# Moving a retention kernel's first operand work partly to GpSimd and giving weight conversions a tick per stage

## The chip, the cores and the metric

The kernel runs on one core of a Trainium2 chip. Its engines are TensorE (PE in the rows, with PEld for its weight loads), VectorE (DVE), ScalarE (ACT), GpSimd (POOL) and SyncE (SP), which here only issues DMAs. The metric is the device time of one execution in microseconds, the median of several runs.

## The reference

Three computations follow each other. First a retention layer with decay, 4 batches, 8 heads, 768 positions, head width 64; then two feed-forward layers over the 3072 resulting rows, one with a leaky ReLU and one with a sigmoid-gated activation:

```python
state = gamma * state + k[:, :, t] (x) v[:, :, t]      # for t in range(768)
y[:, :, t] = scale * q[:, :, t] @ state
x = y as (3072, 512)
h = x @ w_in;  x = maximum(0.01 * h, h) @ w_out        # 512 -> 2048 -> 512
h = x @ w2_in; x = h / (1 + exp(-1.702 * h)) @ w2_out
```

The weights come as float32 widened to 64 bits per element with the value spread over two 32-bit words, so the kernel puts each weight together on the chip before it uses it.

## The kernel before, in words

**Retention.** The 768 positions of a batch are six chunks of 128, so there are 24 steps `s` (last batch first). A step loads one megabyte of q, k and v (`a_load`, four places in turn), multiplies scores (`a_scores`: 16 matmuls at line 741, then one VectorE product with the mask at line 744), scales the keys in eight ScalarE instructions (`a_decay`, line 752), runs the products with the values and the state (`a_out`, lines 764 to 777, state update at 780) and puts the result into SBUF times the query decay (`a_store`, lines 790 and 799). `retention()` is a generator with two halves per step. The first seven steps (`N_PRO`) run alone, with `early(s)` behind each; the other 17 are fed, half a step per tick, into the first 31 ticks of the first layer.

**The layers.** Each layer has two classes. `First` does the product with `w_in` as a seven-product scheme on blocks of 384 columns: four blocks `blk`, eight weight slots `q`, seven products of six matmuls each (line 371). A product is one tick. `Second` does the product with `w_out` (line 596). The order is `first1`, `second1`, `first2`, `second2`. Each product takes one operand form of the block (`First.form`: for forms 3 and 6 a difference in `tmp`, then a rounded copy on ScalarE at line 345, then the remainder on VectorE at line 151). `early_sums` (lines 332 and 333) makes the sum `tmp` and the block difference that forms 5 and 7 need.

**Weights.** `Prep` handles half a slot: `load` (two DMAs of 256 KB, line 203 or 206), `open` (two ScalarE conversions, lines 168 and 169), three VectorE word steps (lines 172, 174 and 176), `round_up` (an integer add on GpSimd, line 185), `total` (three VectorE subtractions: one 128x256, two 128x128, line 151), and then either `keep` (split into the slot: ScalarE copy, line 154, VectorE remainder) or `store` (line 226). The first two slots of the second layer's `w_in` are split and stored as two parts (`split`, `store_split`, lines 234 and 235).

**Order.** All engines run their instructions in program order, and the program order is written by hand. `Later` holds steps by tick: `clock.at(n, step)` puts `step` behind the instructions of the n-th tick from now. `OWN_AT` gives the ticks of the sixteen `1i` preparations (each slot `q` is first needed at tick 7q up to q = 5, then at 39 and 46); `OPEN1` and `OPEN2` give the ticks at which the stored preparations begin. Raw words have two places in turn in the first ticks, then three (`prep_rings[0]`); prepared halves have three (`prep_rings[1]`), and a `split` takes a second one. `behind1` is a queue of weight splits that is worked off one per tick. Activated blocks leave through a ring of buffers `first1.g`, stored by ScalarE's DMA queue at line 383; this ring has four buffers when n is 26 or 27.

Before, the early work is VectorE's:

```python
for n, words in enumerate(EARLY_PREPS):                 # (3, 4)
    if s == words:
        own[n].own_words(later, 1, 2)                   # open + words + round_up, total, keep
...
        first1.form(0, i, (0, 0, 1), e=nc.vector)       # forms 1, 2, 5, 6 at s = 3, 4, 5, 6
...
    first1.early_sums(nc.vector)                        # s == 5
```

Of the kernel before, what the change touches and what calls it, by code (L numbers as in the profile page):

```python
# [25 lines left out]
NC = S // P  # L26
# [12 lines left out]
def _word(bits):  # L39
# [18 lines left out]
N_PRO, N_SINGLE, N_IN1 = 7, 5, 10  # L58
EARLY_LOADS = (0, 3, 4)
EARLY_PREPS = (3, 4)  # L60
EARLY_FORMS = ((1, 3), (2, 4), (5, 5), (6, 6))
OWN_AT = {2: (None, 0, 1, 2), 3: (None, 2, 1, 2), 4: (3, 6, 1, 2), 5: (5, 8, 1, 2), 6: (8, 11, 1, 2), 7: (12, 15, 1, 2),
          8: (16, 19, 1, 2), 9: (20, 23, 1, 2), 10: (23, 26, 1, 5), 11: (26, 29, 1, 3), 12: (28, 31, 1, 3),
          13: (30, 34, 2, 4), 14: (32, 37, 2, 4), 15: (35, 41, 2, 3)}
FED = [2 if k in (10, 18, 26) else 1 for k in range(31)]
OPEN1 = (*range(54, 100, 5), *range(109, 157, 5), *range(165, 195, 5))
OPEN2 = (10, 16, 22, 28, 34, 39, *range(53, 100, 8), *range(109, 158, 8), 165, 173, 181)
# [31 lines left out]
def retention_two_ffn(ctx: ExitStack, tc: tile.TileContext, qkv, consts, small, w1i, w1o, w2i, w2o, scratch, out):  # L99
# [50 lines left out]
    def subtract(o, x, y, e=nc.vector):  # L150
        e.tensor_tensor(out=o, in0=x, in1=y, op=ALU.subtract)  # L151

    def split(hi, lo, src, eng=nc.vector):
        nc.scalar.copy(out=hi, in_=src)
        subtract(lo, src, hi.bitcast(F32), eng)
# [31 lines left out]
    class Prep:  # L187
# [52 lines left out]

        def own_words(self, clock, total, keep):
            self.open()
            self.word(3)
            round_up(self.f, self.low, nc.gpsimd)
            clock.at(total, lambda: self.total(nc.vector))
            clock.at(keep, self.keep)

# [4 lines left out]
        def plan(self, clock, at, lead, keep=False):  # L252
            clock.at(at - lead, self.load)
            clock.at(at, self.open)
            clock.at(at + 1, lambda: self.word(2))
            clock.at(at + 2, self.last_word)
            clock.at(at + 4, lambda: self.total(nc.vector))
            if keep:
                clock.at(at + 6, self.keep)
            elif self.kind == "2i" and self.q < N_SPLIT:  # L260
                clock.at(at + 5, self.split)
                clock.at(at + 7, self.store_split)
            else:
                clock.at(at + 5, self.store)

# [429 lines left out]
    first1.load(0)  # L695

    def early(s):

        for n, words in enumerate(EARLY_PREPS):
            if s == words:  # L700
                own[n].own_words(later, 1, 2)
        if s in EARLY_LOADS:
            own[EARLY_LOADS.index(s) + 1].load()
        for i, k in EARLY_FORMS:
            if s == k:
                first1.form(0, i, (0, 0, 1), e=nc.vector)
        if s == NC - 1:
            first1.early_sums(nc.vector)
        later.tick()

    def retention():
# [103 lines left out]
        a_load(3)  # L815
        own[0].load()
        nc.vector.memset(idle, 0.0)
        first = few.view(3.5, 8)
# [11 lines left out]
        a_decay(0)  # L830
        a_decay(1)
        for s in range(len(steps)):
            if s == 0:
                keep_warm(6)
            elif s + 1 < len(steps):
                a_scores(s + 1)
            yield
            o = a_out(s)
            if s == 0:
                a_scores(1)  # L840
                keep_warm(6)
            put = a_store(s, o)
            if s + 2 < len(steps):
                a_decay(s + 2)
            n = s + 4 if s < 15 else s + 3
            if s != 15 and n < len(steps):
                a_load(n)
            if put is not None:
                put()
            yield  # L850
# [7 lines left out]
    behind1 = collections.deque()  # L858
    for k, i in enumerate(FORMS[4:]):
        first1.form(0, i, (2 * k, 2 * k, 2 * k + 1), e=nc.vector)  # L860
    for n, (load, words, total, keep) in OWN_AT.items():
        if load is not None:
            later.at(load, own[n].load)
        later.at(words, lambda p=own[n], a=total, b=keep: p.own_words(later, a, b))

    todo1 = names["1o"] + names["2i"][2 * N_SPLIT : N_IN1] + names["2i"][: 2 * N_SPLIT]
    assert len(todo1) <= len(OPEN1)
    for p, at in zip(todo1, OPEN1):
        p.plan(later, at, 7)

# [17 lines left out]

    def done_first(kind, second, clock, behind):
        def done(blk, q):  # L890
            if blk < 3:
                return
            if q < NQ - 2:
                w_load(kind, q, 3, 7)
                w_load(kind, q, 0, 3)
                clock.at(6, lambda: behind.extend(w_steps(q, 3, 7) + w_steps(q, 0, 3)))
                return
            w_load(kind, q, 6, 7)
            second.loads(3 if q == NQ - 2 else 5)

        return done

    first1.run(done_first("1o", second1, later, behind1), step1, behind1, chunks, N_SINGLE, FED)
    while behind1:
# [69 lines left out]
    for p, at in zip(todo, OPEN2):  # L974
        p.plan(later2, at, 5, p.kind == "2i")

# [7 lines left out]

    first2.run(done_first("2o", second2, later2, behind), step2, behind)
    while behind:
# [127 lines left out]
```

## Time and profile before

| | us |
|---|---|
| median of 3 runs | 1101.69 (1100.98 to 1101.76) |
| profiled execution, its own time | 1103.22 |
| span of that execution, first to last instruction | 1101.5 |
| PE busy | 1041.2 (95%) |
| DVE busy | 823.8 (75%) |
| ACT busy | 620.1 (56%) |
| POOL busy | 139.6 (13%) |

The profiled execution spends 1.7 us outside its span and is 1.5 us longer than the median of the runs. In that execution the seven lone retention steps last until about 40 us, the fed steps until about 150, `first1` until 390, `second1` until 619, `first2` until 867, and `second2` to the end. A busy share is an average over these stages, so each stage is read by itself. PE's busy time also counts matmuls that run at a lower granted clock.

### The profile page before, as it was taken

What the parts mean: (1) busy time and instruction counts of PE and PEld (TensorE: products, weight loads), DVE (VectorE), ACT (ScalarE), POOL (GpSimd) and SP (SyncE); (2) the same over time, 40 slices, a digit from 0 to 9 for tenths busy, and PEclk for the clock granted to TensorE, in tenths of its full rate; (3) what the DMA queues carried; (4) which work ended last, traced back from release to release, by engine and by line L of the source; (5) the groups of instructions that cost most, each with busy time, mean ns of one, the idle gap of its engine ahead of it and who ended that gap; (6) DMA issues with size and microseconds to landing.
All of it is one profiled execution on the core that took longest, in us unless ns stands there. A gap on an engine that the chain in (4) does not pass through costs nothing.

```text
span 1101.5 us, 17557 instructions
## 1 busy us (share of the span) xinstructions
PE 1041.2 (95%) x6150; PEld 925.6 (84%) x6151; DVE 823.8 (75%) x1351; ACT 620.1 (56%) x1223; POOL 139.6 (13%) x97
## 2 busy tenths in 40 slices
PE   8788988999996999999999998999999999999998
PEld 5567778899996978888888997999999888888886
DVE  5987676778685679788788776556575699798886
ACT  4564654566575655455455665555567655544543
POOL 0110023333331000000000012232220000000000
PEclk9899998999998999999999998999999999999999
DMA  9679954787979873632726673766779752834724
GB/s 341 210 240 329 289 184 136 240 294 255 357 241 340 270 250 96 201 106 86 253 82 228 217 256 124 252 222 225 253 232 326 240 183 63 220 103 111 195 77 77
DMA packets 190568, 231.37 MB, mean 210 GB/s; under 512 B 59152, under 2 KB 146192, under 8 KB 187408
## 3 DMA queue, kind: packets, MB, share of 16 engines
q1 hardware_dynamic: 148704, 179.08, 51.7%
q10 hardware_dynamic: 41776, 51.17, 13.0%
q8 instruction: 48, 0.79, 0.3%
q14 instruction: 40, 0.33, 0.1%
HBM read 141.46 MB, written 88.74 MB: 209 GB/s over the span
## 4 chain that ended last, share of the span: by engine, by line
PE 61%; DMA 14%; DVE 14%; ACT 4%; issue 2%; POOL 2%; SPq 1%; ACTq 1%; POOLq 0%; DVEq 0%
PE psum L596 39%; PE psum L371 20%; DMA w<-qkv 5%; DVE e L151 3%; DVE c L151 2%; DVE w L151 2%; POOL c L185 1%; DMA e<-w2o 1%; DMA e<-w2i 1%; DMA wd2o<-ex 1%; DVE ex L151 1%; PE psum L741 1%; DMA ex<-w2i 1%; DMA wds<-c 1%; DMA ex<-w1o 1%
## 5 line engine op out<-in xcount | busy, mean ns | idle before, releaser
L596 PE MATMUL psum<-c,w 128*128 128x512 f32 x1008 | 229.0, 389 | 0.0
L596 PEld LDWEIGHTS psum<-c,w 128*128 128x128 f32 x1008 | 189.1, 188 | 39.5 <-DVE c L151 0.2
L596 PE MATMUL psum<-e,w 128*128 128x512 f32 x576 | 136.1, 389 | 0.0
L371 PE MATMUL psum<-a,w 128*128 128x384 f32 x576 | 115.4, 350 | 18.5 <-ACT psum L476 8.9
L596 PEld LDWEIGHTS psum<-e,w 128*128 128x128 f32 x576 | 108.0, 188 | 22.9 <-DVE e L151 0.5
L371 PEld LDWEIGHTS psum<-a,w 128*128 128x128 f32 x576 | 104.4, 196 | 23.2 <-ACT psum L476 10.6
L371 PE MATMUL psum<-c,w 128*128 128x384 f32 x576 | 112.9, 339 | 5.9 <-DVE d L400 4.5
L371 PE MATMUL psum<-b,w 128*128 128x384 f32 x576 | 111.1, 336 | 0.4 <-ACT psum L476 0.4
L371 PEld LDWEIGHTS psum<-c,w 128*128 128x128 f32 x576 | 101.6, 190 | 8.5 <-DVE d L400 6.3
L371 PEld LDWEIGHTS psum<-b,w 128*128 128x128 f32 x576 | 101.6, 189 | 0.8 <-ACT psum L476 0.7
L549 ACT CAST c<-b 128x512 fp32r<-128x512 f32 x96 | 59.5, 622 | 55.7 <-DVE c L151 30.3
L151 DVE TENSOR_TENSOR c<-c 128x256 f32<-128x256 f32 (+2 forms) x130 | 62.0, 477 | 37.6 <-POOL c L185 28.5
L371 PE MATMUL psum<-d,w 128*128 128x384 f32 x384 | 78.9, 349 | 8.2 <-DVE w L151 5.0
L371 PE MATMUL psum<-e,w 128*128 128x384 f32 x384 | 77.3, 345 | 6.5 <-DVE dx L400 2.4
L151 DVE TENSOR_TENSOR c<-b,c 128x512 fp32r<-128x512 f32 x96 | 65.6, 690 | 20.1 <-ACT c L549 18.1
L371 PEld LDWEIGHTS psum<-d,w 128*128 128x128 f32 x384 | 68.9, 194 | 12.3 <-DVE w L151 6.0
L371 PEld LDWEIGHTS psum<-e,w 128*128 128x128 f32 x384 | 68.4, 193 | 10.5 <-DVE dx L400 3.4
L390 ACT ACTIVATE d<-psum 128x384 f32<-128x384 f32 x96 | 46.9, 489 | 50.7 <-PE psum L371 46.4
L151 DVE TENSOR_TENSOR w<-w 128x512 fp32r<-128x512 f32 (+3 forms) x102 | 50.3, 529 | 32.7 <-ACT w L285 26.2
L185 POOL TENSOR_TENSOR c<-c,c 128x512 int32<-128x512 int32 x33 | 48.0, 1456 | 210.0 <-DVE c L176 172.0
L549 ACT CAST e<-a 128x512 fp32r<-128x512 f32 x58 | 35.9, 622 | 33.2 <-PE psum L596 14.2
L752 ACT ACTIVATE w<-w,f 128x64 f32<-128x64 f32 x160 | 40.4, 335 | 24.7 <-DMA w<-qkv 19.5
(188 smaller groups left out, 1709.2 us busy)
## 6 DMA issues: line engine op xcount, KB each, us to landing
gd<-d ACTq DMA_DIRECT2D x128, 192.0 KB, 3.5
w<-qkv SPq DMA_DIRECT2D x21, 1024.0 KB, 7.4
b<-gd SPq DMA_DIRECT2D x72, 256.0 KB, 4.3
d<-gd SPq DMA_DIRECT2D x54, 256.0 KB, 3.7
a<-gd SPq DMA_DIRECT2D x48, 256.0 KB, 5.5
gd<-dx ACTq DMA_DIRECT2D x47, 192.0 KB, 4.5
c<-w1i SPq DMA_DIRECT2D x32, 256.0 KB, 4.8
e<-w2o SPq DMA_DIRECT2D x32, 256.0 KB, 5.1
```

What stands on the lines that cost most here:

```text
L151: e.tensor_tensor(out=o, in0=x, in1=y, op=ALU.subtract)
L185: e.tensor_tensor(out=f.bitcast(I32), in0=f.bitcast(I32), in1=low.bitcast(I32), op=ALU.add)
L371: nc.tensor.matmul(out=t, lhsT=w[:, k, a], rhs=x[:, b, k], start=(start and m == 0), stop=(m == 5), skip_group_check=True)
L390: nc.scalar.activation(out=t, in_=x, func=self.func)
L549: nc.scalar.copy(out=t[:, 0], in_=self.block_of(*item))
L596: nc.tensor.matmul(out=t[:, j], lhsT=w[:, j, a], rhs=x[:, b], start=(new and q == 0 and m == 0), stop=(q == NQ - 1 and m == 2), skip_group ...
L741: nc.tensor.matmul(out=ps[:, e, n], lhsT=kT[r, n], rhs=qT[r, n], start=True, stop=True, skip_group_check=True)
L752: nc.scalar.activation(out=ks_t[s][:, h], in_=ks_t[s][:, h], func=AF.Copy, scale=kdec[:, c, h : h + 1])
```

## The change

**Early work.** `own[0]` and `own[1]` are both loaded ahead of the loop, `own[2]` and `own[3]` at steps 5 and 6 (before: steps 0, 3 and 4 for 1, 2 and 3). `open` comes a step ahead of the words. The two `total`s go to GpSimd, as do the remainders of forms 1 and 2 (`low_on_gpsimd`), the block difference of `early_sums` and the difference for form 6. Forms 7, 4 and 3 follow in that order, and the difference for form 3 goes to GpSimd (the default engine of `form`).

**Own preparations.** `OWN_AT` has five columns: load, open, words, total, keep, each at its own tick. Words come one tick behind `open`.

**Stored preparations.** The load lies 10 ticks ahead of `open` instead of 7 in the first layer, 8 instead of 5 in the second. `total` and `store` come one tick later (those with `keep` are unchanged). `OPEN1` has eleven preparations every 4.5 ticks in each of its first two runs (before: ten, every 5), and the last four, those with a split, every 8 ticks instead of 5.

**Keys.** `a_decay(s + 1)` stands behind the scores of step s + 1, where `a_decay(s + 2)` stood at the end of step s.

**Reloads.** The splits of reloaded `1o` weights are queued 9 ticks behind their load instead of 6.

```diff
-EARLY_LOADS = (0, 3, 4)
-EARLY_PREPS = (3, 4)
-EARLY_FORMS = ((1, 3), (2, 4), (5, 5), (6, 6))
-OWN_AT = {2: (None, 0, 1, 2), 3: (None, 2, 1, 2), 4: (3, 6, 1, 2), 5: (5, 8, 1, 2), 6: (8, 11, 1, 2), 7: (12, 15, 1, 2),
-          8: (16, 19, 1, 2), 9: (20, 23, 1, 2), 10: (23, 26, 1, 5), 11: (26, 29, 1, 3), 12: (28, 31, 1, 3),
-          13: (30, 34, 2, 4), 14: (32, 37, 2, 4), 15: (35, 41, 2, 3)}
+OWN_AT = {2: (None, 1, 2, 3, 4), 3: (None, 3, 4, 5, 6), 4: (3, 6, 7, 8, 9), 5: (5, 8, 9, 10, 11), 6: (8, 11, 12, 13, 14),
+          7: (12, 15, 16, 17, 18), 8: (16, 19, 20, 21, 22), 9: (20, 23, 24, 25, 26), 10: (22, 25, 26, 27, 31),
+          11: (25, 27, 28, 29, 32), 12: (27, 30, 31, 32, 34), 13: (29, 33, 34, 36, 38), 14: (32, 36, 37, 39, 42),
+          15: (35, 40, 41, 43, 45)}
-OPEN1 = (*range(54, 100, 5), *range(109, 157, 5), *range(165, 195, 5))
+OPEN1 = (*(54 + 9 * k // 2 for k in range(11)), *(109 + 9 * k // 2 for k in range(11)), 165, 173, 181, 189)
...
-        def own_words(self, clock, total, keep):
-            self.open()
+        def own_words(self):
             self.word(3)
             round_up(self.f, self.low, nc.gpsimd)
-            clock.at(total, lambda: self.total(nc.vector))
-            clock.at(keep, self.keep)
...
-            clock.at(at + 4, lambda: self.total(nc.vector))
             if keep:
+                clock.at(at + 4, lambda: self.total(nc.vector))
                 clock.at(at + 6, self.keep)
-            elif self.kind == "2i" and self.q < N_SPLIT:
-                clock.at(at + 5, self.split)
-                clock.at(at + 7, self.store_split)
+                return
+            clock.at(at + 5, lambda: self.total(nc.vector))
+            if self.kind == "2i" and self.q < N_SPLIT:
+                clock.at(at + 6, self.split)
+                clock.at(at + 8, self.store_split)
             else:
-                clock.at(at + 5, self.store)
+                clock.at(at + 6, self.store)
...
+    def low_on_gpsimd(i):
+        a = {1: (0, 0), 2: (0, 1)}[i]
+        t = first1.at["f"][i][0].view(first1.at["f"][i][1], 2, 2, T1)
+        first1.of[0, i] = t
+        split(t[:, 0], t[:, 1], first1.block(*a), nc.gpsimd)
+
     def early(s):
 
-        for n, words in enumerate(EARLY_PREPS):
-            if s == words:
-                own[n].own_words(later, 1, 2)
-        if s in EARLY_LOADS:
-            own[EARLY_LOADS.index(s) + 1].load()
-        for i, k in EARLY_FORMS:
-            if s == k:
-                first1.form(0, i, (0, 0, 1), e=nc.vector)
-        if s == NC - 1:
-            first1.early_sums(nc.vector)
+        if s == 2:
+            own[0].open()
+        if s == 3:
+            own[0].own_words()
+            own[0].total(nc.gpsimd)
+            own[1].open()
+            low_on_gpsimd(1)
+        if s == 4:
+            own[1].own_words()
+            own[1].total(nc.gpsimd)
+            low_on_gpsimd(2)
+        if s == 5:
+            own[2].load()
+            a, tmp = first1.block, first1.tmp
+            nc.vector.tensor_tensor(out=tmp, in0=a(1, 0), in1=a(1, 1), op=ALU.add)
+            own[0].keep()
+            first1.form(0, 5, (0, 0, 1), e=nc.vector)
+            subtract(a(1, 0), a(1, 0), a(0, 0), nc.gpsimd)
+        if s == 6:
+            own[1].keep()
+            own[3].load()
+            first1.form(0, 6, (0, 0, 1), e=nc.gpsimd)
         later.tick()
...
         own[0].load()
+        own[1].load()
...
         a_decay(0)
-        a_decay(1)
         for s in range(len(steps)):
             if s == 0:
                 keep_warm(6)
             elif s + 1 < len(steps):
                 a_scores(s + 1)
+            if s + 1 < len(steps):
+                a_decay(s + 1)
             yield
...
-            if s + 2 < len(steps):
-                a_decay(s + 2)
...
-    for k, i in enumerate(FORMS[4:]):
-        first1.form(0, i, (2 * k, 2 * k, 2 * k + 1), e=nc.vector)
+    for i, at in ((7, (0, 0, 1)), (4, (1, 1, 2)), (3, (1, 3, 4))):
+        first1.form(0, i, at)
...
-        p.plan(later, at, 7)
+        p.plan(later, at, 10)
...
-                clock.at(6, lambda: behind.extend(w_steps(q, 3, 7) + w_steps(q, 0, 3)))
+                clock.at(ticks, lambda: behind.extend(w_steps(q, 3, 7) + w_steps(q, 0, 3)))
...
-    first1.run(done_first("1o", second1, later, behind1), step1, behind1, chunks, N_SINGLE, FED)
+    first1.run(done_first("1o", second1, later, behind1, 9), step1, behind1, chunks, N_SINGLE, FED)
...
-        p.plan(later2, at, 5, p.kind == "2i")
+        p.plan(later2, at, 8, p.kind == "2i")
...
-    first2.run(done_first("2o", second2, later2, behind), step2, behind)
+    first2.run(done_first("2o", second2, later2, behind, 6), step2, behind)
```

## Rows read from the trace of the kernel before

**Rows 1.** Windows: stretch, length, each engine's busy us, granted clock, DMA share, GB/s.

```profile
27.00:62.00 35.00, 23.23 (x277) 18.67 (x272) 31.14 (x49) 21.75 (x58) 5.95 (x4) 0.85 0.62 211
62.00:150.00 88.00, 80.81 (x1027) 66.98 (x1026) 61.87 (x106) 46.32 (x128) 9.78 (x7) 0.96 0.89 286
150.00:182.00 32.00, 23.74 (x101) 21.71 (x102) 24.62 (x40) 15.55 (x27) 13.21 (x7) 0.83 0.46 148
182.00:390.00 208.00, 190.91 (x1059) 186.11 (x1059) 147.96 (x260) 130.37 (x257) 55.39 (x36) 0.98 0.81 276
390.00:619.00 229.00, 229.00 (x1012) 189.49 (x1011) 192.81 (x303) 122.15 (x207) 2.15 (x1) 1.00 0.49 163
619.00:867.00 248.00, 240.69 (x1352) 236.59 (x1351) 155.69 (x266) 153.73 (x304) 51.81 (x37) 0.98 0.71 237
```

**Rows 2.** Timeline 27 to 48 us: start, length, engine, line, operands [idle before, releaser].

```profile
31.51 2.03 DVE L151 TENSOR_TENSOR c<-c 128x256 f32<-128x256 f32 x3
33.46 0.95 DVE L151 TENSOR_TENSOR d<-b,d 128x768 fp32r<-128x768 f32 x1
...
35.60 2.08 PE L741 MATMUL psum<-w 64*128 64x128 f32 x16 [4.51 <-DVE w L744]
...
43.59 1.08 DVE L151 TENSOR_TENSOR w<-c,w 128x896 fp32r<-128x896 f32 x1
...
46.57 0.83 ACT L345 CAST a<-b 128x768 fp32r<-128x768 f32 x1 [4.80 <-DVE b L151]
```

**Rows 3.** Timeline 55 to 62 us, the first ticks.

```profile
55.84 0.83 ACT L345 CAST e<-b 128x768 fp32r<-128x768 f32 x1 [2.79 <-DVE b L151]
...
57.27 0.43 DVE L172 TENSOR_SCALAR c<-c 128x512 f32<-128x512 f32 x1 [1.47 <-ACT c L168]
...
61.56 1.83 PE L371 MATMUL psum<-a,w 128*128 128x384 f32 x6 [4.60 <-DVE psum L400]
```

**Rows 4.** Timeline 167 to 173 us, VectorE and GpSimd side by side.

```profile
167.55 2.66 POOL L332 TENSOR_TENSOR b<-b 128x768 f32<-128x768 f32 x1
...
168.46 4.21 DVE L151 TENSOR_TENSOR c<-c 128x256 f32<-128x256 f32 x3
```

**Rows 5.** Groups of GpSimd instructions: count, busy us, mean ns, idle before.

```profile
L185 POOL TENSOR_TENSOR ex<-ex,e 128x512 int32<-128x512 int32 x11 | 14.3, 1301 | 64.4 <-DVE ex L176 29.3 <-DMA gd<-d 23.0 <-ACT d L390 12.1
...
L332 POOL TENSOR_TENSOR a<-a 128x768 f32<-128x768 f32 x3 | 5.5, 1832 | 0.0
```

**Rows 6.** Timeline 105 to 156 us, the fed ticks and their end.

```profile
109.87 2.02 ACT L752 ACTIVATE w<-w,f 128x64 f32<-128x64 f32 x8 [6.23 <-DMA w<-qkv]
109.98 2.08 PE L741 MATMUL psum<-w 64*128 64x128 f32 x16 [2.51 <-DMA w<-qkv]
...
151.48 1.08 DVE L151 TENSOR_TENSOR c<-c 128x256 f32<-128x256 f32 x3 [1.47 <-POOL c L185]
...
153.69 1.80 PE L371 MATMUL psum<-a,w 128*128 128x384 f32 x6 [2.50 <-DVE psum L400]
```

**Rows 7.** Timeline 218 to 222 us.

```profile
218.65 0.67 ACT L168 ACTIVATE c<-ex 128x512 f32<-128x512 f32 x1 [3.96 <-DMA ex<-w1o]
...
220.75 1.34 PE L371 MATMUL psum<-e,w 128*128 128x384 f32 x6 [1.37 <-DVE f L400]
```

**Rows 8.** Timeline 339 to 360 us, ScalarE and then TensorE.

```profile
339.99 0.49 ACT L390 ACTIVATE f<-psum 128x384 f32<-128x384 f32 x1 [3.90 <-DMA gd<-f]
...
352.94 0.94 ACT L154 CAST c<-c 128x896 fp32r<-128x896 f32 x1 [4.63 <-DMA wds<-c]
...
344.78 4.20 PE L371 MATMUL psum<-a,w 128*128 128x384 f32 x12 [4.77 <-ACT psum L476]
...
357.23 2.35 PE L371 MATMUL psum<-a,w 128*128 128x384 f32 x12 [3.04 <-ACT psum L476]
```

**Rows 9.** Timeline 663 to 674 us, VectorE and then TensorE.

```profile
663.86 4.22 DVE L151 TENSOR_TENSOR e<-e 128x256 f32<-128x256 f32 x3 [1.47 <-POOL e L185]
...
671.54 2.29 PE L371 MATMUL psum<-c,w 128*128 128x384 f32 x6 [3.76 <-DVE d L400]
```

More of the change, by code (lines that the diff above doesn't have):

```diff
@@ L858, in retention_two_ffn @@
     behind1 = collections.deque()
-    for k, i in enumerate(FORMS[4:]):
-        first1.form(0, i, (2 * k, 2 * k, 2 * k + 1), e=nc.vector)
-    for n, (load, words, total, keep) in OWN_AT.items():
+    for i, at in ((7, (0, 0, 1)), (4, (1, 1, 2)), (3, (1, 3, 4))):
+        first1.form(0, i, at)
+    for n, (load, opened, words, total, keep) in OWN_AT.items():
+        p = own[n]
         if load is not None:
-            later.at(load, own[n].load)
-        later.at(words, lambda p=own[n], a=total, b=keep: p.own_words(later, a, b))
+            later.at(load, p.load)
+        for at, step in ((opened, p.open), (words, p.own_words), (total, lambda p=p: p.total(nc.vector)), (keep, p.keep)):
+            later.at(at, step)
     todo1 = names["1o"] + names["2i"][2 * N_SPLIT : N_IN1] + names["2i"][: 2 * N_SPLIT]
@@ L887, in step1, with done_first @@
             second1.begin(later, 0, NQ, 4, 24, 3)
-    def done_first(kind, second, clock, behind):
+    def done_first(kind, second, clock, behind, ticks):
         def done(blk, q):
```

## The prediction

> **What bounds the kernel now.** I read the windows by stage first. In the second product of the first layer, 390 to 619 us, TensorE is never idle and its clock is full; nothing the change does to other engines can shorten that stretch, and the same code runs again behind 867. What can be won lies in the first products. Window length less TensorE's busy time gives its idle time: 11.8 us in 27 to 62, 7.2 in 62 to 150, 8.3 in 150 to 182, 17.1 in 182 to 390, 7.3 in 619 to 867 [rows 1]. Beside that the granted clock averages 0.85, 0.96, 0.83, 0.98 and 0.98, a mix of its two levels, 1.2 and 2.4 GHz; one minus it, times the length, is 5.3, 3.5, 5.4, 4.2 and 5.0 us. These are ceilings for each stage.
>
> Next the timeline, for who ends each wait. From 27 to 62 us VectorE is busy 31.14 of 35 us [rows 1]: the lone retention steps are bound by VectorE's order. The first `total` takes 2.03 us there, form 1's remainder 0.95 us, and only then comes the mask product on which TensorE waits 4.51 us. The last split of slot 0 begins on VectorE at 43.59, and form 6's copy on ScalarE idles 4.80 us for a VectorE difference [rows 2]. In the first ticks form 3's copy waits 2.79 us in the same way, the words of own[3] wait 1.47 us for their own `open`, and behind both stands the add for which TensorE waits 4.60 us [rows 3]. In the fed stage DMA is 0.89 busy [rows 1], and at 110 us TensorE and ScalarE both stand at a q, k, v load, 2.51 and 6.23 us [rows 6].
>
> **The change, part by part.**
>
> *Lone steps.* Taken off VectorE ahead of the split at 43.59: two `total`s, 2.03 [rows 2] and 1.08 (the same shape, undisturbed) [rows 6]; two remainders of 0.95 and one block difference of that shape, 2.85 [rows 2]. Sum 5.96 us. Ahead of form 6's copy one more difference goes, 0.95.
>
> What GpSimd pays: its 512-column add takes 1.30 us, its 768-column one 1.83 [rows 5], so 0.53 per 256 columns; by that line a `total` (256, 128, 128 columns) is an estimated 0.77 + 0.50 + 0.50 = 1.77 us. Two of those, four 768-column operations and the two old integer adds make 2 x 1.77 + 4 x 1.83 + 2 x 1.30 = 13.5 us. Begun near 27 us, form 6's difference would end at 40.5 undisturbed; its copy began at 46.57 before [rows 2]. So GpSimd, slow as it is, has 6 us to spare.
>
> The disturbance is the question. While GpSimd ran its sums at 167.55 (2.66 us instead of 1.83), VectorE's three subtractions took 4.21 us instead of 1.08 [rows 4 to 6]: 3.1 us on one side and 0.8 on the other. About six VectorE operations with two SBUF operands stay in these steps (two word steps, the sum, two splits, one remainder). Bounds: undisturbed, the gain is 5.96, and up to 2 us of the low clock with it, 8 in all; if each of the six waits a whole 1.83 us operation, 11 us are lost, so -5. I take 2 us of disturbance, nearer the undisturbed end, since VectorE spends most of these steps on products that read PSUM, and none of those is among the disturbed rows: **4.0**.
>
> The Trainium skill, in "SBUF — State Buffer", section "Who interferes with whom", states the reason: VectorE and GpSimd share a port pair as an exclusive lock, and a VectorE instruction with two SBUF inputs is fully blocked by a GpSimd one that reads SBUF, and the reverse. This trace agrees, with 4.21 us beside 1.08 [rows 4, 6]. Taken at its hardest (all six blocked) the rule would make this term -5 and the whole sum 7.5 instead of 16.5; it speaks against the change, and the first rival below prices a milder form from rows.
>
> *First ticks.* In front of the add before 61.56 go form 3's difference (0.95), the wait for `open` (1.47) and the split of own[2], now two ticks later (1.08); form 4's remainder comes in (0.95). 3.50 - 0.95 = **2.5** of the 4.60 [rows 2, 3]; bounds 0 and 4.6. What is late next is that split, needed only at tick 7.
>
> *Keys and q, k, v.* The eight scalings (2.02 us [rows 6]) now stand behind the scores, which need the same load, so ScalarE no longer waits for a load ahead of TensorE. They must be done two to three ticks later; ScalarE is 46.32 of 88 us busy [rows 1], which covers them. Own[1]'s load goes ahead of step 4's; the bytes are the same. Own[4] to own[6] now load one tick behind the integer add that frees their place: SP can stand about an add and its hand-over (1.5 us) in front of later q, k, v loads. Where TensorE waits for DMA itself nothing is won. Value **1.0**, bounds -2 (one scaling late) and 4.
>
> *Own preparations 10 to 15.* VectorE stood 1.47 us for GpSimd's add, then TensorE 2.50 us for VectorE's [rows 6]. With `open` a tick ahead the words start up to 1.47 us sooner [rows 3]. Against it own[15]'s split moves from tick 44 to 45, just ahead of its product at 46: copy 0.94 [rows 8] and remainder 1.08 [rows 2], less half a product under way, 1.4 us at most. Value **2.0**, bounds -1.4 and 8.3, the idle time there.
>
> *Stored preparations, first layer.* ScalarE waits 3.96 us for a late load, and TensorE 1.37 us behind it [rows 7]; three more ticks of lead remove that, and the later `total` removes VectorE's stand for GpSimd. The raw place is freed at tick +2 of a preparation and loaded at +3.5, so SP may stand, with nothing urgent behind it. Value **1.5**, bounds 0 and 4.
>
> *The four splits.* With three places and two per preparation, a split 5 ticks behind the last needs a place whose store has not landed: ScalarE waits 4.63 us, then TensorE 3.04. Eight ticks remove it. The larger wait, 4.77, stands behind a 3.90 us wait for a buffer of `first1.g` [rows 8], whose four places the change leaves alone. Value 3.04 and 1 of the disturbance around it, **4.0**; bounds 0 (if the ring takes over) and 7.8.
>
> *Reloads 9 ticks behind:* fewer ScalarE stands, but some splits fall behind the last product; **0.5**, bounds -1 and 1. They are covered by the first five products of `second1`, which need other slots.
>
> *Second layer.* Half of the 7.3 us idle is one wait, 3.76 us, that follows a `total` of 4.22 us [rows 9]. That preparation is kept, its ticks unchanged, and the block sums still stand right behind its integer add, so it recurs. Earlier loads and the later `total` for the stored ones: **1.0**, bounds -1 and 2.5.
>
> Sum: 4.0 + 2.5 + 1.0 + 2.0 + 1.5 + 4.0 + 0.5 + 1.0 = 16.5 us. From the profiled execution's 1103.2 that is 1086.7; it ran 1.5 us above the median of the runs, so the median comes to **1085**.
>
> **The rivals.**
>
> *The port gives the first gain back.* GpSimd's long operations block VectorE's splits as at 168 us; two such collisions of 3.1 us eat the first term, and form 3's difference, 0.9 us slower on GpSimd, with another eats the second. 10 us remain: 1092. For it: VectorE has little slack in that window; against: GpSimd has 6 us to spare.
>
> *More than the sum.* TensorE keeps its high clock through the lone steps and through 150 to 182, and the ring wait falls with the splits: first term 8, fourth 6, sixth 6, together 10 more: 1075. For it: both low-clock stretches hold long idles; against: part of the idle there has other releasers.
>
> *Hidden anyway.* The fed stage is paced by q, k, v loads, so an earlier start is given back by 150 us, and the store ring keeps the wait at 345. The last two terms remain, less a microsecond: 1101.
>
> *Slower: keys in front of TensorE.* ScalarE runs late in the fed ticks, the scalings now come one half step closer to the products that need them, and TensorE waits. Fourteen of the fed steps scale keys. At 1.5 us each that is 21 us, and with the other terms 1107; it decides against the change from 1.1 us a step (15.5 over 14). For it: ScalarE stood up to 6.23 us in its order there [rows 6]; against: that stand was for the load itself.
>
> **How the numbers follow.** Forecast 0.40, own range 1080 to 1090; port 0.22; more 0.12; hidden 0.10; slower 0.16. Differences under 0.2%, 2.2 us, cannot be told from none here. Faster: 0.40 + 0.22 + 0.12 + 0.02 of hidden = 0.76; same 0.08; slower 0.16. The range from 1071 to 1104 leaves out nearly all of the slower case and a little below the fast one.
>
> **What would show it.** Right: the split that began at 43.59 begins near 39.5; no 4.5 us wait for the mask product; the wait at 61.56 near 2; scalings never the releaser of TensorE; no wait for the split stores; the 3.76 us wait still there. Wrong: VectorE groups of 3 to 4 us beside GpSimd in 27 to 45; TensorE released by the key scalings; a new long wait of SP that a q, k, v load stands behind; an unchanged end of the fed stage.

## The result, and the profile after

The kernel after takes 1091.14 us (median of 5 runs, 1089.19 to 1093.86), beside 1100.98 for the kernel before (5 runs, 1099.04 to 1101.76): a ratio (after over before) of 0.9912, with an interval of 0.9892 to 0.9932. That is 9.8 us won where 16.5 were forecast. 1085 was named; 1091 lies inside the whole range (1071 to 1104), 1 us outside the forecast's own (1080 to 1090), and nearest to the 1092 of the port rival. So the number alone would speak for that rival; the runs below have to decide.

The two profiled executions stand wider apart than the medians: 1103.22 before, 2.2 above its median, and 1089.19 after, 2.0 below its own. So 14.0 us lie between the two traces, and 9.8 between the kernels. The windows of after by stage (same columns as [rows 1]; the borders follow the stages, which now begin a little earlier):

```profile
27.00:60.00 33.00, 26.60 (x330) 21.71 (x323) 28.61 (x41) 18.16 (x48) 17.88 (x14) 0.83 0.65 211
60.00:147.00 87.00, 76.64 (x1005) 63.24 (x1005) 64.15 (x111) 47.86 (x137) 11.69 (x9) 1.00 0.90 297
147.00:178.00 31.00, 21.43 (x122) 18.54 (x119) 23.16 (x36) 15.33 (x26) 10.45 (x6) 0.94 0.50 160
178.00:380.00 202.00, 190.92 (x1060) 186.06 (x1061) 144.60 (x256) 127.64 (x252) 55.80 (x36) 0.98 0.81 281
380.00:609.00 229.00, 229.00 (x1013) 189.50 (x1012) 194.15 (x306) 124.41 (x212) 1.87 (x1) 1.00 0.50 165
609.00:853.00 244.00, 237.74 (x1351) 235.59 (x1350) 152.80 (x266) 153.17 (x304) 52.77 (x37) 0.99 0.72 240
```

TensorE's idle time in the lone steps fell from 11.8 to 6.4 us, and GpSimd's work there rose from 5.95 to 17.88. In `first1` (178 to 380) the idle time is 11.1 where it was 17.1. The second product of the first layer is what it was, 229.00 us, as it had to be.

Windows hide where a stage loses and wins again. For that I matched TensorE's matmuls of the two traces in order and took the difference of their start times (after minus before; minus is earlier), at points given by the time before:

```
before, us     16    24   47.5    64   148   180   330   390   660  1095
after, us    +0.6  +3.3  +1.2  -3.3  -2.0  -3.2  +2.5  -9.7  -9.9 -14.0
```

After is 3.3 us late by 24 us, wins 6.5 by 64, loses 5.7 between 180 and 330, wins 12.2 between 330 and 390, and 4.1 in the second layer. Two of the stretches are losses that the forecast had as nothing or as a gain. The timeline of after (columns as in [rows 2]) at the first of them and in the lone steps:

```profile
22.97 1.16 PE L756 MATMUL psum<-w 64*128 64x128 f32 x16 [3.20 <-DMA w<-qkv]
...
33.93 1.99 POOL L149 TENSOR_TENSOR d<-b,d 128x768 fp32r<-128x768 f32 x1
34.29 2.18 DVE L174 SCALAR_TENSOR_TENSOR c<-c,c 128x512 uint32<-128x512 uint32 x1
...
37.65 1.57 PE L756 MATMUL psum<-w 64*128 64x128 f32 x16 [3.15 <-DVE w L759]
...
42.89 1.81 POOL L149 TENSOR_TENSOR b<-b 128x768 f32<-128x768 f32 x1
43.63 2.03 DVE L149 TENSOR_TENSOR w<-c,w 128x896 fp32r<-128x896 f32 x1 [0.32 <-ACT w L152]
46.67 1.81 POOL L149 TENSOR_TENSOR b<-b 128x768 f32<-128x768 f32 x1 [1.96 <-DVE d L149]
48.51 0.83 ACT L342 CAST a<-b 128x768 fp32r<-128x768 f32 x1 [4.92 <-POOL b L149]
...
59.08 1.31 PE L368 MATMUL psum<-a,w 128*128 128x384 f32 x6
```

TensorE stands 3.20 us for a q, k, v load at 22.97. The mask product's wait is 3.15 instead of 4.51 [rows 2]. The split of 43.59 begins at 43.63, not earlier, and takes 2.03 us instead of 1.08, with a GpSimd operation beside it; form 6's copy comes at 48.51, 1.9 us later than before, now behind GpSimd, whose difference at 46.67 had waited 1.96 us for a VectorE remainder. At 59.08 stands the product that waited 4.60 us [rows 3]: it waits no more.

In `first1` and at the start of `first2`, same view:

```profile
206.66 1.25 SPq L320 DMA_DIRECT2D b<-xd  x1
208.00 0.38 SPq L224 DMA_DIRECT2D wd1o<-c  x1
...
219.19 0.66 ACT L166 ACTIVATE c<-c 128x512 f32<-128x512 f32 x1 [6.66 <-DMA c<-w1o]
...
221.30 1.32 PE L368 MATMUL psum<-a,w 128*128 128x384 f32 x6 [2.00 <-DVE psum L397]
...
272.51 0.59 SPq L320 DMA_DIRECT2D b<-xd  x1
273.20 0.38 SPq L224 DMA_DIRECT2D wd1o<-c  x1
...
283.12 0.66 ACT L166 ACTIVATE c<-ex 128x512 f32<-128x512 f32 x1 [4.81 <-DMA wd1o<-c]
...
338.95 0.49 ACT L387 ACTIVATE dx<-psum 128x384 f32<-128x384 f32 x1 [2.50 <-DMA gd<-dx]
342.40 0.94 ACT L152 CAST c<-c 128x896 fp32r<-128x896 f32 x1 [0.57 <-DMA wds<-c]
346.57 1.31 PE L368 MATMUL psum<-e,w 128*128 128x384 f32 x6 [1.68 <-DVE dx L397]
...
661.86 1.47 PE L368 MATMUL psum<-c,w 128*128 128x384 f32 x6 [4.00 <-DVE d L397]
```

ScalarE still stands for a DMA at 219.19, 6.66 us where it was 3.96 [rows 7]. The row names a load, but the load that this `open` needs had landed at 210.6, and the next one landed only from 220.7 on. What landed just ahead of it, at 219.12, is the store issued at 208.00, 11.1 us after its issue: it stands in SyncE's queue (SPq) right behind the 1.5 MB load of the next block's input (`b<-xd`). At 283.12 the same happens again: the store of 273.20, right behind the block load of 272.51, landed after 9.8 us. The median of such stores in 185 to 330 us is 4.8. The split stores' 4.63 us have become 0.57, and where TensorE had its two long waits [rows 8] none over 1.68 is left; even ScalarE's wait for the `gd` ring is 2.50 instead of 3.90. The 3.76 us wait of the second layer [rows 9] is there again, 4.00 at 661.86.

### The profile page after: what moved, and what is told of

Same layout as the page of the kernel before. It is cut to its first block, busy times and chain, and to the rows that moved or that the text cites. A ratio compares the mean times of both kernels' runs of the same rounds, so it can differ in the third digit from the quotient of the medians.

```text
span 1087.5 us, 17567 instructions
## 1 busy us (share of the span) xinstructions
PE 1033.8 (95%) x6150; PEld 919.9 (85%) x6151; DVE 815.0 (75%) x1340; ACT 618.2 (57%) x1223; POOL 151.8 (14%) x108
## 4 chain that ended last, share of the span: by engine, by line
PE 65%; DMA 12%; DVE 12%; ACT 4%; issue 3%; POOL 2%; SPq 1%; ACTq 1%; POOLq 0%; DVEq 0%
PE psum L593 40%; PE psum L368 23%; DMA w<-qkv 3%; DVE c L149 2%; DMA gd<-dx 2%; DMA c<-w1i 2%; DMA c<-w1o 2%; POOL c L183 2%; DVE e L149 1%; DVE w L149 1%; DVE c L174 1%; DMA b<-xd 1%; DVE c L170 1%; ACT w L152 1%; DMA w<-wd1o 1%
## 5 line engine op out<-in xcount | busy, mean ns | idle before, releaser
L593 PEld LDWEIGHTS psum<-c,w 128*128 128x128 f32 x1008 | 189.1, 188 | 39.5 <-DVE c L149 0.2
L368 PE MATMUL psum<-a,w 128*128 128x384 f32 x576 | 112.4, 344 | 6.5 <-DVE psum L397 3.6
L368 PEld LDWEIGHTS psum<-a,w 128*128 128x128 f32 x576 | 101.8, 192 | 11.3 <-ACT psum L473 4.7
L368 PE MATMUL psum<-d,w 128*128 128x384 f32 x384 | 79.6, 350 | 11.1 <-ACT w L152 6.8
L149 DVE TENSOR_TENSOR c<-c 128x128 f32<-128x128 f32 (+1 forms) x124 | 59.0, 476 | 31.5 <-POOL c L183 24.2
L183 POOL TENSOR_TENSOR c<-c,c 128x512 int32<-128x512 int32 x33 | 45.2, 1369 | 189.4 <-DVE c L174 142.5
L149 POOL TENSOR_TENSOR a<-a 128x768 f32<-128x768 f32 x7 | 14.0, 2001 | 276.1 <-DVE b L149 276.1
```

What stands on the lines that cost most here:

```text
L183: e.tensor_tensor(out=f.bitcast(I32), in0=f.bitcast(I32), in1=low.bitcast(I32), op=ALU.add)
L368: nc.tensor.matmul(out=t, lhsT=w[:, k, a], rhs=x[:, b, k], start=(start and m == 0), stop=(m == 5), skip_group_check=True)
L593: nc.tensor.matmul(out=t[:, j], lhsT=w[:, j, a], rhs=x[:, b], start=(new and q == 0 and m == 0), stop=(q == NQ - 1 and m == 2), skip_group ...
```

## The experiments

All versions compute the whole reference. Each was timed beside the kernel before; the ratio is taken over all runs and need not be the quotient of the two medians, and its interval is some 2 us to either side (up to 3.6 where a kernel had six runs). So each run's place in the matched order of matmuls is read as well. That place is of one execution, and it can lie far from its kernel's median: 7.1 us above it for the second layer's part, 8.4 above for own[1] late, 6.0 below for GpSimd's work on VectorE.

**One part at a time.** The first four runs put one part each into the kernel before. Keys scaled a step later, alone:

```
-        a_decay(1)                     # ahead of the steps
+            if s + 1 < len(steps): a_decay(s + 1)     # behind a_scores(s + 1)
-            if s + 2 < len(steps): a_decay(s + 2)     # behind a_store(s, o)
```

> The kernel before with only the keys scaled a step later. Theory (the scalings wait for a load that the scores need too, so nothing is won and the cover is long): within 1.5 us of before, no wait of TensorE with the scalings as its releaser. Rival (the scalings come too close to the products that need them): 10 us or more slower, in the fed ticks. A third reading, that ScalarE no longer standing for loads is the source of the gain: 3 to 5 us faster by 150 us.

1100.08 beside 1101.92, ratio 0.9991 (0.9971 to 1.0011): nothing that can be told from none. No wait of TensorE has the scalings as its releaser. The slower rival, 21 us on this part, is out.

Stored preparations of the first layer, alone:

```
-OPEN1 = (*range(54, 100, 5), *range(109, 157, 5), *range(165, 195, 5))
+OPEN1 = (*(54 + 9*k//2 for k in range(11)), *(109 + 9*k//2 for k in range(11)), 165, 173, 181, 189)
-p.plan(later, at, 7)
+p.plan(later, at, 10)            # total and store at +5, +6; reloads 9 ticks behind
```

> The kernel before with only the first layer's stored preparations changed (eleven every 4.5 ticks, splits every 8, loads 10 ticks ahead, total and store a tick later, reloads 9 ticks behind). Theory (the closer spacing makes opens wait for stores and loads, the wider splits remove the waits near 345 and 357 us): 5 to 7 us lost between 220 and 325 us, 9 to 11 us won between 335 and 390, so 3 to 5 us faster in all. Rival (the loss between 220 and 325 seen in the changed kernel came with the shifted start): no loss there, 9 us or more faster.

1097.57 beside 1101.92, ratio 0.9963 (0.9942 to 0.9984). In its trace 180 to 330 loses 4.5 us and 330 to 390 wins 10.6: the loss and the gain of after both belong to this part, and neither needs the earlier start. ScalarE's list of waits, 185 to 335 us (total, count, longest), suggested a cause, stores that land late:

```profile
ACT c L168 <- DMA wd1o<-c: 13.3, 6, 5.5
```

Stored preparations of the second layer, alone (load 8 ticks ahead instead of 5, `total` and `store` a tick later):

```
-p.plan(later2, at, 5, p.kind == "2i")
+p.plan(later2, at, 8, p.kind == "2i")
```

> The kernel before with only the second layer's preparations changed (loads 8 ticks ahead, total and store a tick later). Theory (the later total takes VectorE's stand for GpSimd away from small waits at three places): 2 to 3.5 us faster, the 3.8 us wait near 671 us still there. Rival (the second layer's difference between the two traces is scatter): within 1 us of before.

1096.98 beside 1101.92, ratio 0.9947 (0.9925 to 0.9968), more than the 1 us that it was given. From 660 to the end its trace wins 2.8. It shows something else too: up to 619 us its code is that of before, yet between 110 and 148 us it falls 5.3 behind. The windows 110 to 148 of before, then of this kernel:

```profile
110.00:148.00 38.00, 34.39 (x424) 28.92 (x424) 23.73 (x40) 20.32 (x60) 3.86 (x3) 0.96 0.87 270
```

```profile
110.00:148.00 38.00, 31.90 (x364) 26.68 (x364) 22.98 (x38) 19.02 (x57) 3.84 (x3) 0.90 0.80 254
```

Less DMA, more idle time and a lower granted clock, with the same instructions: what one trace shows of the fed stage can be off by 5 us. (The keys' kernel loses 4.1 in 64 to 148 as well, and its execution was 5.6 us above its median.)

The early work, alone (GpSimd's part, the ticks of `OWN_AT`, own[1]'s load ahead of the steps). It is after with the rest taken back:

```
-OPEN1 = (*(54 + 9*k//2 ...), 165, 173, 181, 189)   +OPEN1 = (*range(54, 100, 5), ...)
-p.plan(later, at, 10)   +p.plan(later, at, 7)       # total, store, reloads, keys as before too
```

> The kernel before with only the early work on GpSimd, the own preparations' stages in their own ticks and the load of own[1] ahead. Theory (the port lock and the load ahead of step 4's eat the gain of the lone steps, the first ticks gain about 4 us): the first product of the tick stage begins 1 to 2 us later than before, by 64 us it stands 3 us ahead, by 180 us 3 to 4 us ahead; 3 to 4 us faster in all. Rival (the keys are part of it: ScalarE stands for loads in front of opens and copies): 0 to 1 us faster alone.

1097.46 beside 1101.92, ratio 0.9954 (0.9932 to 0.9976). It is 3.1 us late by 24, as after is (3.3), and 4.5 early by 64.

**One part taken out of after.** Own[1]'s load back behind step 0:

```
         own[0].load()
-        own[1].load()
...
+        if s == 0: own[1].load()
```

> The changed kernel with the load of own[1] behind the loads of step 4 again, at step 0. Theory (that load ahead of step 4's q, k, v delays the scores of step 4, 2 to 3 us in both runs that have it): the products of 21 to 27 us come 2 us earlier, the first tick 1 to 2 us earlier, 1 to 2 us faster in all. Rival (VectorE and GpSimd bound the lone steps, the loads do not): the scores come earlier, the first tick does not.

The loss at 24 us is gone (-0.2 instead of +3.3). The product that waited 3.20 us in after, in this kernel's timeline:

```profile
20.68 1.16 PE L758 MATMUL psum<-w 64*128 64x128 f32 x16 [1.64 <-DMA w<-qkv]
```

The last split of slot 0 now begins at 40.01, and 64 us is reached 7.8 us early. In this trace all of it is gone by 148 (+0.4). The time cannot be told from after's: ratio 0.9908 (0.9875 to 0.9941). The q, k, v loads in its list of TensorE's waits, 60 to 150 us:

```profile
PE psum L758 <- DMA w<-qkv: 8.4, 4, 3.0
```

In after they take 7.6 us of that stretch, hardly less, so they alone don't tell where it went. The windows 62 to 148, after and then this kernel, show more:

```profile
62.00:148.00 86.00, 76.07 (x1005) 62.76 (x1005) 62.44 (x108) 46.86 (x130) 11.69 (x9) 1.00 0.90 298
```

```profile
62.00:148.00 86.00, 75.31 (x911) 62.59 (x910) 58.50 (x103) 43.95 (x124) 10.35 (x8) 0.92 0.85 279
```

TensorE is busy as long, but at a granted clock of 0.92 instead of 1.00, and gets fewer matmuls done. How much of that is the scatter just shown stays open: this execution was 8.4 us above its kernel's median. The two later kernels with this edit lose 3.8 and 3.1 in 64 to 148, where after loses 1.3; but the kernel with lead 7, further below, which has own[1]'s load ahead, loses 3.8 there too. That the fed stage takes the gain back is likely from these, and not shown.

GpSimd's new work on VectorE, all else as in after:

```
-own[0].total(nc.gpsimd)          +own[0].total(nc.vector)       # own[1] likewise
-low_on_gpsimd: split(..., nc.gpsimd)   +split(..., nc.vector)
-form(0, 6, ..., e=nc.gpsimd)     +form(0, 6, ..., e=nc.vector)  # block difference and form 3's likewise
```

> The changed kernel with all the work that it moves to GpSimd (two totals, two remainders, the differences for forms 3, 6 and 7) on VectorE, order and ticks as they are. Theory (GpSimd's long operations and the port give back what VectorE saves): the split of own[1] within 1.5 us of the changed kernel's, in all within 1.5 us. Rival (GpSimd carries the gain of the early work): the split 4 us later and the kernel 4 us slower than the changed one.

1097.55 beside 1100.40, ratio 0.9974 (0.9954 to 0.9993): by the medians some 6 us of after's gain are GpSimd's. Its timeline:

```profile
32.26 1.08 DVE L149 TENSOR_TENSOR c<-c 128x256 f32<-128x256 f32 x3 [1.45 <-POOL c L183]
...
35.39 2.08 PE L756 MATMUL psum<-w 64*128 64x128 f32 x16 [4.39 <-DVE w L759]
...
49.10 1.08 DVE L149 TENSOR_TENSOR w<-c,w 128x896 fp32r<-128x896 f32 x1
```

The undisturbed split takes 1.08 again, but begins 5.5 us later than in after, and the mask product's wait is back at 4.39. By 64 us this trace is where before's was (+0.1), 3.4 us behind after's; from there on it wins as much as after's, and 1 us more. So the trace gives GpSimd 3.4 us where the medians give 6, with the trace's execution 6.0 below its median; the size is open between the two. One thing more: from 47.5 to 64 it wins 5.3 us, as after does (4.5). What the first ticks win is thus not GpSimd's, but that of the new order and ticks.

**What loses in 180 to 330.** Three theories: the longer lead of the loads puts them in front of others; the stores, a tick later, leave no margin before the prepared half's place is used again; the closer spacing (two more preparations there) simply costs. Lead 7 instead of 10:

> The changed kernel with loads of the first layer's stored preparations 7 ticks ahead again. Theory (the opens wait because a prepared half's place is reused 13.5 ticks after its open and stored at tick 6, so 7.5 ticks stay for the store, whatever the loads do): opens still wait 5 us or more for stores between 180 and 330, late loads come back, time within 2 us of the changed kernel, rather above it. Rival (loads ten ticks ahead stand in SP's queue in front of the stores and make them late): the waits for stores are gone and it is 4 us or more faster than the changed kernel.

Still +4.7 in 180 to 330, ratio 0.9913 (0.9892 to 0.9934). The lead is not it, nor, at this spacing, a gain.

Spacing 5, so 20 preparations instead of 22 there:

```
+OPEN1 = (*range(54, 100, 5), *range(109, 157, 5), 165, 170, 176, 182, 188, 194)
```

> The changed kernel with the stored preparations every 5 ticks again (twice ten), two more at 165 and 170 and the four splits 6 ticks apart from 176. Theory (the close spacing leaves too little time for the stores): no wait of an open for a store over 1 us between 180 and 325, 4 to 6 us won there; the splits wait a little again, 1 to 4 us lost of the 9; in all 1 to 5 us faster than the changed kernel. Rival (the later total and store cost it, not the spacing): the loss between 220 and 325 stays, and with the nearer splits it is slower than the changed kernel.

180 to 330 now wins 2.6 instead of losing 5.7, and 330 to 390 wins 3.0 instead of 12.2. The list of TensorE's waits, 325 to 395 us, and ScalarE's split ahead of the long one show what is back:

```profile
PE psum L368 <- DVE dx L397: 6.9, 2, 6.5
...
348.71 0.94 ACT L152 CAST c<-c 128x896 fp32r<-128x896 f32 x1 [5.08 <-DMA wds<-c]
```

The time is the same: ratio 0.9910 (0.9879 to 0.9942). This run changes two things, the spacing of the preparations and that of the splits, which are 6 ticks apart here and 8 in after. The split of 348.71 waits 5.08 us for the store of an earlier one, as before's waited 4.63; so what is lost again behind 330 need not be the price of the two preparations that now stand there.

Store and `total` a tick earlier (first layer), for the margin of the store:

```
-clock.at(at + 5, lambda: self.total(nc.vector))    +clock.at(at + 4, ...)
-clock.at(at + 6, self.store)                       +clock.at(at + 5, self.store)
```

> The changed kernel with total and store of the first layer's stored preparations at ticks 4 and 5 again (split at 5, its store at 7); the spacing of 4.5 and all else stay. Theory (a prepared half's place is stored too shortly ahead of its reuse: one more tick for the store): waits of opens for stores halve, the loss between 180 and 330, 5 to 6 us in the changed kernel against before, falls to 2 to 4; the end of the stage unchanged. Rival (the spacing costs for another reason, VectorE and ScalarE have too much work per tick): the loss stays at 5 us or grows.

This was my favoured theory, and it fell: 180 to 330 loses 8.5 us, and the ratio is 0.9977 (0.9955 to 0.9999), most of after's gain gone by the median of twelve runs. VectorE's waits for GpSimd's add, 182 to 328 us: before, after, spacing 5, this kernel:

```profile
DVE c L151 <- POOL c L185: 20.1, 17, 1.5
```

```profile
DVE c L149 <- POOL c L183: 15.0, 14, 1.5
```

```profile
DVE c L149 <- POOL c L183: 10.8, 9, 1.5
```

```profile
DVE c L149 <- POOL c L183: 25.3, 21, 1.5
```

With the `total` early VectorE stands behind the add 21 times at up to 1.5 us, and everything queued behind it on VectorE stands too. The store behind the block load takes up to 10.4 us to land here too, so a tick more did not cover it. At this spacing the later `total` and store are worth having; `total` and store were moved together, and which of them counts is not shown. The next kernel has them early again, stands 18 times (20.0 us), and yet keeps after's time.

A mixture, after with the early `total` and `store`, own[1] late and

```
+OPEN1 = (*(54 + 19*k//4 for k in range(11)), *(109 + 19*k//4 for k in range(11)), 166, 174, 182, 190)
```

> The changed kernel with the store a tick earlier in the first layer, the stored preparations every 4.75 ticks and the splits from 166, and the load of own[1] back at step 0. Theory (the three costs that the runs showed are separate): no wait of an open for a store over 2 us, 180 to 330 within 2 us of the kernel before, the first tick 3 us earlier than in the changed kernel; 4 to 8 us faster than the changed kernel. Rival (what the early part wins is given back in the fed ticks, where loads set the pace): the same as the changed kernel within 2 us.

0.9896 (0.9870 to 0.9922): not to be told from after, and the 4 to 8 us hoped for are not there. +6.6 in 180 to 330.

Spacing 5, but 22 preparations, and own[1] late:

```
+OPEN1 = (*range(54, 105, 5), *range(109, 160, 5), 167, 175, 183, 191)
```

> The changed kernel with twice eleven stored preparations every 5 ticks (the last of each eleven in the ticks of the next block's forms), the splits 8 apart from 167, and the load of own[1] back at step 0. Theory (the distance of 4.5 ticks costs the loss between 180 and 330, not the number of preparations there): 180 to 330 no slower than in the kernel before, the splits' gain after 330 kept at 8 us or more; faster than the changed kernel by 5 us or more. Rival (two more preparations in that stretch are simply two more to do, and what they cost there the end of the stage has less): 180 to 330 loses 4 us or more again and the time is within 3 us of the changed kernel.

0.9915 (0.9889 to 0.9941). With the wider spacing 180 to 330 still loses 4.6; then 330 to 390 wins 9.3. By the test that was set, that speaks for the number of preparations. But the loss is another one. By before's time after loses 1.8, 1.6 and 2.2 us at 220 to 230, 240 to 250 and 280 to 290; this kernel wins 2.4 at the first of these places and loses nothing at the other two. It loses 4.5 at 255 to 257 and some 5 at 310 to 330. There the eleventh preparation, which spacing 5 with 20 does not have, meets the next block's forms: its add goes ahead of the form's difference on GpSimd, ScalarE's copy waits for that, and TensorE for the copy:

```profile
243.88 1.90 POOL L183 TENSOR_TENSOR c<-c,ex 128x512 int32<-128x512 int32 x1 [5.40 <-DVE c L174]
245.74 1.80 POOL L149 TENSOR_TENSOR b<-b 128x768 f32<-128x768 f32 x1
247.58 0.83 ACT L342 CAST a<-b 128x768 fp32r<-128x768 f32 x1 [3.59 <-POOL b L149]
248.84 3.77 PE L368 MATMUL psum<-a,w 128*128 128x384 f32 x12 [3.15 <-ACT psum L473]
```

What goes with the distance is ScalarE's stand for loads and stores ahead of `open`. Between 185 and 328 us it comes to 13.5 to 15.8 us in the six kernels with 4.5 ticks, whatever lead and store, to 8.5 with 4.75, and to 1.6 and 1.8 with 5, with 20 preparations as with 22; in before, with lead 7, it is 7.0. With spacing 5 the slowest store still takes 9.1 and 9.3 us to land, but no `open` stands for it. So both cost in this stretch, each at its own places: the close distance where a prepared half's place is wanted before the store behind the block load has landed, the eleventh preparation in the next block's forms.

**Which half in the second layer.** Only the later `total` and `store`, the load at 5 ticks as before:

```
-clock.at(at + 4, lambda: self.total(nc.vector))    +clock.at(at + 5, ...)      # later2 alone
-clock.at(at + 5, self.store)                       +clock.at(at + 6, self.store)
```

> The kernel before with only total and store a tick later in the second layer, loads 5 ticks ahead as before. Theory (VectorE's stand for GpSimd's add is what the later total removes): the same small gains at 694, 728, 753, 787, 813 and 840 us as with both edits, 3.4 us between 660 and the end. Rival (the earlier loads are the source): 1 us or less there.

1098.00 beside 1099.64, ratio 0.9969 (0.9951 to 0.9987), and 660 to the end wins 3.9, where both edits won 2.8: the later `total` and store give it without the longer lead. VectorE's waits, 690 to 860 us, before and this kernel:

```profile
DVE e L151 <- POOL e L185: 6.9, 5, 1.5
DVE ex L151 <- POOL ex L185: 5.9, 5, 1.5
```

```profile
DVE ex L151 <- POOL ex L185: 4.9, 4, 1.5
DVE e L151 <- POOL e L185: 3.9, 3, 1.5
```

## Why the prediction was right, and where its sizes were off

Fourteen profiled executions allow a better ledger than two. For each stretch the kernels that have the part stand beside those that have before's code there: the mean change against before's trace, in us, with the standard deviation of the kernels, and the difference beside the term of the sum.

```
stretch      with the part (n)   without (n)   difference   forecast
0-24          +3.4 +-0.2 (6)     +0.7 +-0.9 (8)    +2.7      0 (in "the bytes are the same")
24-47.5       -2.9 +-0.7 (8)     +0.2 +-0.2 (5)    -3.1     -4.0
47.5-64       -4.7 +-0.5 (9)     +0.1 +-0.1 (5)    -4.8     -2.5
64-148        +1.4 +-1.6 (5)     +1.7 +-2.5 (5)    -0.3     -1.0
148-180       -0.9 +-0.5 (9)     -0.3 +-0.8 (5)    -0.5     -2.0
180-390       -4.7 +-2.2 (9)     -1.8 +-1.5 (5)    -2.9     -6.0 (1.5 + 4.0 + 0.5)
660-end       -4.1 +-0.9 (10)    -0.5 +-0.6 (4)    -3.6     -1.0
```

A minus is a gain. The three kernels with own[1] late count as without in 0 to 24 and are left out of 64 to 148; GpSimd's work on VectorE (+1.7 in 24 to 47.5) is left out of 24 to 47.5 and 64 to 148. In 64 to 148 the keys' kernel counts as without and the early work alone as with, so that row does not measure the keys. The nine of 180 to 390 include those whose lead, spacing or store was changed. The differences sum to 12.5 us; since the fed stage alone scatters by 2.5, this doesn't contradict the 9.8 of the medians. The four parts measured alone sum to some 16 (1.8, 4.4, 4.9, 4.5), each within about 2, near the 16.5 of the sum, but together they gave 9.8. Whether they take from each other or the scatter of five differences makes the gap is open.

**Lone steps: mechanism right, one step wrong.** The 3.1 us of 24 to 47.5 lie near the 4.0, and with GpSimd's work on VectorE the same stretch loses 1.7. The disturbance was forecast at 2 us; the word step of 2.18 (0.69 alone) and the split of 2.03 (1.08 alone) make 2.4, and no VectorE group reached the 3 to 4 us named as a sign of being wrong. The mask product's wait was to go and only shrank, to 3.15. The step that failed is "Own[1]'s load goes ahead of step 4's; the bytes are the same". The bytes are the same, but the q, k, v load that they now precede is the one for which TensorE stands 3.20 us at 22.97: 2.7 us lost by 24. Without that step the split begins at 40.01, where 39.5 was forecast. The net term is 0.4 instead of 4.0. The kernels without that step did not come out faster by their medians, so what it costs in the whole time is not shown.

**First ticks.** Mis-sized low: 4.8 instead of 2.5. The whole 4.60 us wait went, not only the operations that left the chain in front of it. It went with form 3's difference on VectorE too, so that piece of the working was not needed.

**The port.** 2.18 and 2.03 us stand beside GpSimd operations, and the split alone takes 1.08; the Trainium skill's rule ("SBUF — State Buffer", "Who interferes with whom") agrees with that. But the rival that prices it, that the port gives the gain back, fell, though its number, 1092, was the nearest: the two stretches whose terms it struck out show 3.1 and 4.8 us, and with the same work on VectorE the kernel is some 6 us slower by the medians. GpSimd's 6 us to spare were not there: form 6's difference ended at 48.48 and not at 40.5, since GpSimd began at 30.67 and not at 27, its operations took up to 2.68 us instead of 1.83, and it waited 1.96 us for VectorE. That it did no harm is luck: form 6's copy came 1.9 us later, and no wait of TensorE stands behind it.

**Keys and q, k, v loads.** Nothing that the median can tell; the 1.0 lies within the scatter. The slower rival, 1.5 us on each of fourteen steps, had no support in the keys' kernel or in after.

**Own preparations.** Forecast 2.0, measured 0.5, which the scatter of 0.5 to 0.8 does not tell from nothing.

**Stored preparations and the four splits.** The step that failed is the sign of "Value 1.5, bounds 0 and 4": 180 to 330 loses 4.5 to 5.7, outside the bounds. I had priced lead and `total` there, and not that the new `OPEN1` puts the preparations 4.5 ticks apart, two more of them into that stretch. With spacing 5 and 20 preparations, lead and `total` as in after, the stretch wins 2.6, inside the bounds. The splits' term is the other side of it: 10.6 to 12.2 between 330 and 390 where 4.0 was forecast. The wait of 4.77, which I left standing behind the ring, went as well, and the two preparations are gone from there; no run tells these two apart. The windows 330 to 390, before and after:

```profile
330.00:390.00 60.00, 48.47 (x261) 46.55 (x261) 36.34 (x67) 36.64 (x76) 5.75 (x4) 0.94 0.88 303
```

```profile
330.00:390.00 60.00, 58.05 (x319) 55.41 (x318) 39.44 (x77) 41.87 (x89) 3.93 (x3) 1.00 0.90 315
```

TensorE's idle time falls from 11.5 to 2.0 us and the granted clock goes from 0.94 to 1.00. Together the stretches give 2.9 where the sum had 6.0 (4.1 by the ratio of that part alone). In 180 to 330 after loses at three places. Two of them follow an `open` that waits for the store behind a block load: 6.66 us at 219.19, behind which TensorE waits 2.00 us at 221.30, and 4.81 us at 283.12, behind which it waits 0.89 us. So the lead did what was forecast, no `open` of after stands for its own load there, and the close distance put a late store in its place. What makes the loss between them is not settled.

**Second layer.** The 3.76 us wait recurs, as forecast. The later `total` (with its store) was undervalued: 3.6 in the ledger instead of 1.0, 3.9 by itself. VectorE stood for the add ten times, 12.8 us, between 690 and 860; with the later `total` seven times, 8.8 us, and the forecast had priced none of these short stands.

**Hidden anyway** may hold for one piece: what own[1] late wins by 64 us is back by 148 in its trace, and none of the three kernels with it is faster than after; the scatter of that stage leaves this unproven. It did not hold for the rest of the early gain: the early work alone is still 4.3 us early at 180.

No version beats after by more than its interval; the best ratio, 0.9896, is that of the mixture.

## What to carry to other kernels

A load moved ahead of others is priced by the load that it delays, not by its bytes. An instruction that stands behind another engine's result holds up everything queued behind it, so giving it one tick more can be worth more than removing the longest single wait. Where a schedule is spread anew, count what each stretch gains in instances and how soon each place is wanted again, price both stretches together, and look whether two versions that lose alike lose at the same places. Check the releaser that a row names against the time at which that DMA landed. And before a gain in a DMA-paced stage is read from one trace, see how far two executions of the same code lie apart there.

## What the runs showed of the hardware that I had not expected

A store in SyncE's queue right behind a 1.5 MB load took 11.1 and 9.8 us to land in after, where the median of such stores is 4.8. The fed stage, with the same instructions, took 5.3 us more in one execution than in another within 38 us, at a DMA share of 0.80 instead of 0.87 and a granted clock of 0.90 instead of 0.96. And VectorE's operations beside GpSimd grew by less than in the rows before: the word step from 0.69 to 2.18 us and the split from 1.08 to 2.03, where three subtractions had gone from 1.08 to 4.21 [rows 4, 6]. TensorE's wait for the mask product behind that word step still fell, from 4.51 to 3.15, with the work that had left VectorE.
